# Expert buffers in existing rings, an earlier weight pool, a routing chain put out in another order, and first transfers in another order

## The chip, the cores and the metric

One core of one Trainium2 chip runs the whole program in one launch. The metric is the device time of the launch in microseconds (us); lower is better. Three runs of the kernel before gave 870.08, 864.69 and 865.5 us, median 865.5. The profiled execution, from which every row below comes, took 872.73 us, of which the profile's span is 870.9 us; the mean clock granted to TensorE in it was 0.964 of full speed.

## The reference

Attention, a dense MLP and a mixture of experts follow one another:

```python
s_g = scale * q_g @ k_all.T ; out_g = softmax(s_g) @ v_all        # 32 global tokens see all 544
mask = abs(pos[:, None] - pos[None, :]) <= 32                     # 512 local tokens: window and globals
a_l = softmax(concat([scale * q_l @ k_g.T, where(mask, s_ll, -1e9)]))
x = concat([out_g, a_l @ concat([v_g, v_l])])                     # 4 batches, 8 heads, D 64 -> [2176, 512]
h = x @ w_in ; x = (h * sigmoid(h)) @ w_out                       # 512 -> 2048 -> 512
logits = x @ w_gate ; e = argmax(logits) ; p = softmax(logits)[e] # 8 experts
eom = sigmoid(x @ w_output_gate)
out[mask_e] = p * eom[:, e] * (relu(x @ w1[e]) @ w2[e])           # 512 -> 1024 -> 512, one expert a token
```

All inputs and the output are float32.

## The kernel before

**Numbers.** A float32 product is made of three fp16 products: each operand is split into a high and a low half (`wih`/`wil` for w_in, `woh`/`wol` for w_out), scaled by a power of two taken from the sum of its squares. Such a sum is an ACT instruction that writes a tile nobody reads (`junk`) and accumulates on the side (`stat`, L226 to L228).

**Stages.** The 2176 tokens are 17 tiles of 128. Attention of batch 0 goes in float32 (`att0_s`, `att0_v`), since its operands come first and aren't split; batches 1 to 3 are split. Each step of attention computes the scores of one pair of heads, the softmax, the transposes and the product with v; `att_step` puts out one. The MLP works in groups of up to 512 tokens: `mlp_h` (L681) makes x @ w_in, `mlp_x` (L728) the second product. Attention, MLP and the preparation of weights overlap. Behind the MLP of a tile, `x2_evac` writes its split rows to a DRAM tensor `x2d`, transposes them to `x2T`, and `logits` (or `logits32` for the last tiles) computes the gates.

**Routing.** `route` turns logits into lists of rows, on DVE with small matmuls on TensorE: `onehot` and `ranks` number the tokens of each expert; `early_slots` takes the first 128 tokens of each expert among tiles 0 to 14 (`pme` L1124, then the row numbers `idge` L1125), and `last` gives, once all 17 tiles are known, the list `idg` (`pm` L1173, L1174) of 13 more slots of 128 rows whose expert is known only then. Coefficients (`pce`, `pcf`, `coef`), and the list by which results are scattered (`pt`, `ids`), come out of further small products.

**Experts.** `Moe` handles 21 slots of 128 rows in four chunks of 256 hidden units. GpSimd gathers a slot's rows (`gather`, L1241), SP transposes them (L1243), `mm_h` (L1286, L1278, L1281) makes 256 hidden units of a slot in 12 matmuls, ACT and DVE make `hb` of it, SP transposes two slots' `hb` at a time (L1313), and `mm_y` (L1323) adds the second product to `ys` in 6 matmuls. The 13 slots of `last` are gathered by `gather_late`. Weights of a chunk come as 16 tiles `ws` of 512 KB (L918), get a `stat` and are split (L954 on ACT, L955 on DVE).

**What sets the order.** A scheduler of the kernel's framework orders instructions on each engine from the source order, a priority (`tc.high_priority(URG)`) and `tc.issue_after(i)`, which holds back what it encloses until i has been put out. An engine then works in that order and waits at the first instruction whose inputs aren't there. A buffer of a ring (a pool's tag with `bufs=n`) is reused in turn: who takes it waits for the last reader of its predecessor. A pool that opens where another has closed waits for whatever used that memory. In the kernel before, `ws` has 2 buffers until `rt_ctx.close()` and 6 afterwards; the tiles of the late slots, `hb`, `r` and `ys` lie in pools opened behind `mlp_ctx.close()`.

**The start.** L1404 to L1424: SP issues q0, k0, the mask `cs`, q1, the constants `cr` (with the identity by which the softmax is transposed), w_in part 0, v0; then `scale_v0` (an ACT sum over v0, L319, and a tiny product `tot`, L192) stands ahead of the first step of attention.

Of the kernel before, what the change touches and what calls it, by code (L numbers as in the profile page):

```python
# [9 lines left out]
F32 = mybir.dt.float32  # L10
# [42 lines left out]
NEARLY = NE  # L53
ORDER = (*range(14), 16, 14, 15)
# [52 lines left out]
def tile_kernel(ctx: ExitStack, tc, csa, csr, q0, q, qn, qg, k0, k, va, vc, w_in, w_out, wg, w1, w2, out, dbg=None):  # L107
# [89 lines left out]
    woh = wto.tile([128, KF, DM], F16, name="woh")  # L197
    wol = wto.tile([128, KF, DM], F16, name="wol")
# [246 lines left out]
    pt, av, sums, xs = {}, {}, {}, {}  # L445

# [5 lines left out]
    ident = cr[:, C_ID:C_ID + 128]  # L452

# [13 lines left out]
    def att0_s(t, pr):  # L467
# [513 lines left out]
    def route(rt, rps):  # L981
# [9 lines left out]
        DVE.tensor_scalar(trib, iota, cr[:, C_P:C_P + 1], None, ALU.is_gt)  # L991
        ones = T([128, 128], "ones", BF16)
# [43 lines left out]
        apend, pc_i = [], [None]  # L1036
# [55 lines left out]
        def early(i):  # L1092
# [11 lines left out]
            else:  # L1104
# [3 lines left out]
                coef(14, 15)  # L1108

                DVE.tensor_scalar(n0[:, 1], n0[:, 1], 128.0, None, ALU.max)  # L1110
                r, SR = slice(0, 15), [128, 15, NE]
                DVE.tensor_scalar(u[:, r, 0], dhi[:, r], 0.0, None, ALU.is_equal)
                DVE.tensor_tensor(RE, ohf[:, r], bc(u[:, r], SR), ALU.mult)
                static(0, 15)

        def early_slots():
            pump_a(99)
            SR = [128, 15, NEARLY]
            for c in range(2):
                DVE.tensor_tensor(Rce[:, :, c], RE, bc(row[c][:, 0:15], SR), ALU.mult)  # L1120
            pm = rps.tile([128, NEARLY], F32, tag="av", name="pme")
            for i in range(15):
                for c in range(2):
                    PE.matmul(pm, A[:, i], Rce[:, i, c], start=(i == 0 and c == 0), stop=(i == 14 and c == 1))  # L1124
            DVE.tensor_scalar(idge, pm, -1.0, 0.0, ALU.add, ALU.max)  # L1125
# [15 lines left out]
        def last():  # L1141
            p = onehot(15, 17)
            DVE.tensor_tensor(n0[:, 2], n0[:, 1], p[:, 0, 0], ALU.add)
            n1 = T([128, NE, 1], "n1")
            DVE.tensor_tensor(n1[:, :, 0], n0[:, 2], p[:, 0, 1], ALU.add)
            cmp = d.rearrange("p i e -> p (i e)").rearrange("p (e i) -> p e i", e=NE)
            S3t = [128, NE, NT]
            DVE.tensor_tensor(cmp, bc(n1, S3t), bc(cr[:, C_CNT:C_CNT + NT].rearrange("p (a i) -> p a i", a=1), S3t), ALU.is_gt)
            sl = T([128, NE], "sl")
            DVE.tensor_reduce(sl, cmp, AX.X, ALU.add)  # L1150
            DVE.tensor_scalar(sl, sl, -float(NS), 0.0, ALU.add, ALU.max)
            DVE.tensor_tensor_scan(bnd[:, 0], one8, sl, 0.0, ALU.mult, ALU.add)
            base = T([128, 1, NE], "base")
            DVE.scalar_tensor_tensor(base[:, 0], bnd[:, 0], float(ST - NS), sl, ALU.add, ALU.subtract)
            ranks(15, 17, p, n0[:, 1:3])
            static(15, 17)
            S3 = [128, NT, NE]
            DVE.tensor_tensor(tmp, ohf, bc(base, S3), ALU.mult)
            b_ = T([128, NT, 1], "b_")
            DVE.tensor_reduce(b_[:, :, 0], tmp, AX.X, ALU.add)  # L1160
            DVE.tensor_tensor(b_[:, :, 0], b_[:, :, 0], u[:, :, 0], ALU.mult)
            DVE.tensor_tensor(b_[:, :, 0], b_[:, :, 0], dhi, ALU.add)
            SR = [128, NT, NSLOT]
            R = Rc[:, :, 2]
            i24 = iota[:, 0:NSLOT].rearrange("p (a n) -> p a n", a=1)
            DVE.tensor_tensor(R, bc(i24, SR), bc(b_, SR), ALU.is_equal)
            for c in range(2):
                DVE.tensor_tensor(Rc[:, :, c], R, bc(row[c], SR), ALU.mult)
            pump_a(99)
            pm = rps.tile([128, NSLOT], F32, tag="av", name="pm")  # L1170
# [42 lines left out]
    class Moe:  # L1213
# [376 lines left out]
```

## Time and profile before

| | before |
|---|---|
| three runs, us | 870.08, 864.69, 865.5 |
| profiled execution, us | 872.73 (span 870.9) |
| TensorE busy | 769.5 us of the span |
| DVE busy, ACT busy | 590.1 us, 516.8 us |
| first matmul, first step of the MLP, end of the MLP | 16.85, 77.66, 565.1 us |
| chunk 0 of the experts: last `mm_h` | 652.8 us |

Times in the rows are microseconds from the start of the span. PE is TensorE, SPq the queue in which SP issues transfers. A timeline row gives start, duration and count of a run of like instructions, and in brackets the idle time before it with what ended it. The table of windows gives for each stretch the busy time of each engine, the granted clock (1.00 is full speed) and the share of the 16 DMA engines that was busy; as it counts overlapping packets it can go above 1.

### The profile page before, as it was taken

The numbers are of one execution on the slowest core, as the hardware profiler recorded it, in microseconds if no ns is written. First come the engines' busy times: TensorE is split into PE (matmuls) and PEld (weight loads), VectorE is DVE, ScalarE is ACT, GpSimd is POOL, SyncE is SP. The second block draws the span as 40 slices with busy tenths as digits, with TensorE's granted clock in tenths as the row PEclk, the third lists the DMA queues.
The fourth block names the chain that finished last, engine by engine and source line by source line (L and its number), as shares of the span: only waits on it lengthen the run. The fifth ranks groups of instructions, "written<-read, shape, count | busy, mean of one in ns | idle before, by whom it ended". The sixth has DMA issues, their size and how long they took to land.

```text
span 870.9 us, 17387 instructions
## 1 busy us (share of the span) xinstructions
PE 769.5 (88%) x6201; PEld 525.3 (60%) x6201; DVE 590.1 (68%) x1649; ACT 516.8 (59%) x1017; POOL 58.1 (7%) x110
## 2 busy tenths in 40 slices
PE   2999969899899999999999889968759998899894
PEld 2898656566666766677666557545425655455541
DVE  2978876777767878767565556872126787588862
ACT  2685768677667667666545555411359846756710
POOL 0000000000000000000000000035000000000054
PEclk9999888999999999999999999979979999999997
DMA  9733444366974284646354262199975974885672
GB/s 356 292 121 123 150 149 161 107 145 167 183 122 89 48 176 99 137 86 122 67 99 106 95 146 65 46 194 194 197 202 174 237 143 151 181 167 170 141 175 90
DMA packets 182139, 127.83 MB, mean 147 GB/s; under 512 B 161437, under 2 KB 162973, under 8 KB 178592
## 3 DMA queue, kind: packets, MB, share of 16 engines
q1 hardware_dynamic: 178688, 116.67, 55.5%
q0 software_dynamic: 3360, 9.97, 3.9%
q8 instruction: 54, 0.88, 0.4%
q14 instruction: 37, 0.30, 0.1%
HBM read 76.93 MB, written 9.96 MB: 100 GB/s over the span
## 4 chain that ended last, share of the span: by engine, by line
PE 42%; DMA 20%; DVE 14%; issue 9%; ACT 9%; SPq 2%; POOL 1%; POOLq 0%; ACTq 0%; DVEq 0%
PE h L681 10%; PE x L728 10%; DMA ws<-in_w_dram 6%; PE yp L1323 5%; DMA pT<-pb 4%; DMA wil<-hb 4%; PE hp L1286 3%; PE av L531 2%; PE s L475 2%; DMA st<-in_qn_dram 2%; DVE w1b L955 2%; DVE k L210 2%; PE av L497 1%; PE av L498 1%; ACT w1b L954 1%
## 5 line engine op out<-in xcount | busy, mean ns | idle before, releaser
L728 PE MATMUL x<-woh,g 128*128 128x512 f16 x544 | 173.5, 381 | 0.3 <-ACT g L711 0.3
L681 PE MATMUL h<-xT,wih 128*128 128x256 f16 (+1 forms) x1152 | 162.0, 272 | 3.6 <-DMA xT<-xb 1.5
L681 PEld LDWEIGHTS <-wih 128*128 128x128 f16 x1152 | 109.3, 100 | 29.5 <-issue 4.7
L728 PEld LDWEIGHTS <-g 128*128 128x128 f16 x816 | 76.3, 98 | 80.4 <-issue 2.6
L1323 PE MATMUL yp<-w2b,wil 128*128 (+1 forms) x384 | 93.4, 390 | 19.5 <-DMA wil<-hb 11.9
L728 PE MATMUL x<-wol,g 128*128 128x512 f16 x272 | 103.8, 382 | 0.0
L1286 PE MATMUL hp<-w1b,x 128*128 128x256 f16 (+1 forms) x672 | 87.8, 279 | 8.9 <-DMA x<-xg 4.7
L681 PE MATMUL h<-xT,wil 128*128 128x256 f16 (+1 forms) x576 | 87.3, 273 | 0.0
L1286 PEld LDWEIGHTS <-x 128*128 128x128 f16 x672 | 67.0, 101 | 27.6 <-issue 5.9
L464 ACT ACTIVATE e<-e,mx,esc 128x192 f32<-128x192 f32 (+1 forms) x128 | 70.5, 553 | 19.1 <-DVE mx L461 17.5
L228 ACT ACTIVATE junk<-ws 128x1024 f16<-128x1024 f32 x48 | 50.8, 1058 | 41.5 <-DMA ws<-in_w_dram 40.8
L1323 PEld LDWEIGHTS <-wil 128*128 128x128 f16 x384 | 38.0, 102 | 61.4 <-issue 13.4
L683 ACT ACTIVATE tanh<-h,th 128x512 f32<-128x512 f32 (+1 forms) x72 | 47.1, 658 | 41.9 <-PE h L681 41.7
L700 ACT ACTIVATE g<-tanh,i_out 128x512 f16<-128x512 f32 (+1 forms) x64 | 44.1, 692 | 33.8 <-DVE tanh L696 33.7
L681 PEld LDWEIGHTS <-wil 128*128 128x128 f16 x576 | 55.4, 100 | 7.2 <-issue 0.2
L701 DVE SCALAR_TENSOR_TENSOR g<-tanh,i_out,g 128x512 f16<-128x512 f32 (+1 forms) x64 | 45.7, 716 | 20.5 <-ACT g L700 20.3
L696 DVE SCALAR_TENSOR_TENSOR tanh<-tanh,h 128x512 f32<-128x512 f32 (+1 forms) x64 | 41.4, 649 | 26.6 <-ACT tanh L683 26.3
L460 DVE CUSTOM_DVE_ANT_0 e<-s,cs 128x192 f32<-128x192 f32 (+1 forms) x128 | 42.7, 370 | 19.7 <-PE s L450 11.0
L955 DVE SCALAR_TENSOR_TENSOR w1b<-ws,s,w1b 128x1024 f16<-128x1024 f32 x32 | 40.1, 1280 | 14.1 <-ACT w1b L954 14.0
L955 DVE SCALAR_TENSOR_TENSOR w2b<-ws,s,w2b 128x1024 f16<-128x1024 f32 x32 | 40.6, 1282 | 12.0 <-ACT w2b L954 9.5
L516 DVE SCALAR_TENSOR_TENSOR pb<-e,pb 128x384 f16<-128x384 f32 (+1 forms) x48 | 28.0, 587 | 18.6 <-ACT pb L515 18.2
L514 POOL MEMSET pb<- 128x256 f16 (+1 forms) x48 | 12.4, 259 | 360.9 <-DMA pT<-pb 144.6
(345 smaller groups left out, 1395.1 us busy)
## 6 DMA issues: line engine op xcount, KB each, us to landing
ws<-in_w_dram SPq DMA_DIRECT2D x64, 512.0 KB
st<-in_w_out_dram SPq DMA_DIRECT2D x8, 1024.0 KB
st<-in_w_in_dram SPq DMA_DIRECT2D x6, 1024.0 KB
q<-in_q_dram SPq DMA_DIRECT2D x12, 512.0 KB
x2d<-x2s SPq DMA_DIRECT2D x17, 256.0 KB
st<-in_k_dram SPq DMA_DIRECT2D x3, 1088.0 KB
st<-in_qn_dram SPq DMA_DIRECT2D x3, 1024.0 KB
st<-in_va_dram SPq DMA_DIRECT2D x3, 1024.0 KB
```

What stands on the lines that cost most here:

```text
L228: ACT.activation(junk, x, ACTF.Square, accum_out=m)
L460: DVE.tensor_tensor_reduce(dst[:, hh, 0:wt], ps[:, hh, 0:wt], mask, 1.0, -3e38, ALU.add, ALU.max, mx[:, hh:hh + 1])
L464: ACT.activation(dst[:, hh, 0:wt], dst[:, hh, 0:wt], ACTF.Exp, scale=esc[:, b:b + 1], bias=mx[:, 2 + hh:3 + hh], accum_out=sums[i][:, h:h ...
L681: PE.matmul(ps[:, f], w[:, kk, c], xj[:, l + kk, 0:n], start=(m == 0 and kk == 0), stop=(m == 2 and kk == KD - 1))
L683: pin[0] = ACT.activation(t, ps, ACTF.Tanh, scale=th[:, b:b + 1])
L696: pin[1] = DVE.scalar_tensor_tensor(t, t, 1.0, ps, ALU.add, ALU.mult)
L700: ACT.activation(hi, t, ACTF.Copy, scale=i)
L701: pin[2] = DVE.scalar_tensor_tensor(lo, t, i, hi, ALU.mult, ALU.subtract)
L728: PE.matmul(x2ps[2 * j + c], x[:, f, o], w[:, ff], start=(ff == 0 and m == 0), stop=(ff == KF - 1 and m == 2))
L955: DVE.scalar_tensor_tensor(d[:, 1], t[a], sc_, d[:, 0], ALU.mult, ALU.subtract)
L1286: PE.matmul(ps[:, 0], x[:, xl + kk], self.rows("1", n, l, kk), start=(m == 0 and kk == 0), stop=(m == 2 and kk == KD - 1))
L1323: PE.matmul(ps, h[:, hl + j], self.rows("2", n, l, j), start=(m == 0 and j == 0), stop=(m == 2 and j == KJ - 1))
```

## The change

- **Start.** The mask and k0 come in parts, w_in part 0, `cr` and the first half of v0 are issued ahead of w_in part 1, q1 and the rest; `scale_v0` is put out behind the fourth step of attention.
- **Weights.** `ws` has 6 buffers from the end of attention on, and six of the eight w1 tiles of chunk 1 are asked for ahead of the routing of the last tiles (`prefetch(wq1)`).
- **Memory.** The MLP's pools stay open. Late rows are gathered into the `xt` and `x2` rings (`room`), transposed into `woh` and `wol` (`xlate`); `ys` of ten late slots share those rings; `hb` and the `junk` of later weights go in the MLP's `g` ring of 6, `r` in its ring of 2 (before: own rings of 2 and 3, and one own `junk`). Routing tables lie in halves of `wil`, `ohs` and `ohb`.
- **Routing.** `early_slots` up to `idge`, and `last` up to `idg`, are put out at high priority; coefficients and the scatter list come behind `idge` and `idg` by `issue_after`.

```diff
 def load_k0():
-        SP.dma_start(kt[0], k0)
+        for h in range(0, 4, 2):
+            SP.dma_start(kt[0][:, h:h + 2], k0[:, h:h + 2])
...
         load_q(0)
+        SP.dma_start(cs[:, 0:WT[0]], csa[:, 0:WT[0]])
         load_k0()
-        SP.dma_start(cs, csa)
+        load_w(("i", 0))
+        SP.dma_start(cr, csr)
+        load_v0()
+        load_w(("i", 1))
         load_q(1)
-        SP.dma_start(cr, csr)
-        load_w(("i", 0))
-        load_v0()
+        SP.dma_start(cs[:, WT[0]:], csa[:, WT[0]:])
+        load_v0_rest()
+        load_w(("i", 2))
...
-        scale_v0()
         while npos[0] < P["n0"]:
             att_step()
+            if npos[0] == 4:
+                with tc.issue_after(sc0[0].ins):
+                    scale_v0()
...
-        def early_slots():
-            pump_a(99)
+        def early_slots():
+            SR = [128, 15, NEARLY]
+            with tc.high_priority(URG):
+                pump_a(99)
...
+                key_i[0] = DVE.tensor_scalar(idge, pm, -1.0, 0.0, ALU.add, ALU.max)
+            with tc.issue_after(key_i[0].ins):
+                DVE.tensor_scalar(n0[:, 1], n0[:, 1], 128.0, None, ALU.max)
+                coef(14, 15)
                 static(0, 15)
...
         def last():
-            p = onehot(15, 17)
+            with tc.high_priority(URG):
+                p = onehot(15, 17)
...
+                key_i[0] = DVE.tensor_scalar(idg, pm, -1.0, 0.0, ALU.add, ALU.max)
+            with tc.issue_after(key_i[0].ins):
+                early_coefs()
...
+        def room(self, k, a):
+            if k < 6:
+                if k % 2 == 0:
+                    self.pair[a] = xt_p.tile([128, 2, DM], F32, tag="xT", name="yx")
+                return self.pair[a][:, k % 2]
+            if k < 10:
+                return x2_p.tile([128, DM], F32, tag=("x2s", "x2T")[k % 2], name="yx")
+            return self.ys_p.tile([128, DM], F32, tag=f"y{k}", name="yx")
+
+        def xlate(self, k):
+            return xlv[k // 8][:, k % 8]
...
-                r = self.pools[1].tile([128, CH], F32, tag="r", name="r")
-                if o == 0:
-                    self.hb[q] = self.pools[1].tile([128, 2, 2, CH], F16, tag="hb", name="hb", bufs=2)
...
+            r = gt_p.tile([128, CH], F32, tag="tanh", name="r")
+            if o == 0:
+                self.hb[q] = g_p.tile([128, 2, 2, CH], F16, tag="g", name="hb")
...
-                    wm["s"], wm["n"] = rt_ctx.enter_context(tc.tile_pool(name="ws", bufs=2, side="right")), 1
+                    wm["s"], wm["n"] = ctx.enter_context(tc.tile_pool(name="ws", bufs=6, side="right")), 3
...
+        wm["j"] = lambda: g_p.tile([128, 1024], F16, tag="g", name="junk")
+        wq1 = [(1, "1", p) for p in range(4)]
+        prefetch(wq1)
         moe.mm_h(0)
...
         rt_ctx.close()
-        mlp_ctx.close()
-
         ys_p = ctx.enter_context(tc.tile_pool(name="ys", bufs=1))
-        xs_p = ctx.enter_context(tc.tile_pool(name="xs", bufs=1))
-        r_p = ctx.enter_context(tc.tile_pool(name="r", bufs=3))
-        wm["s"], wm["n"] = ctx.enter_context(tc.tile_pool(name="ws", bufs=6, side="right")), 3
-        wm["j"] = lambda: xs_p.tile([128, 1024], F16, tag="xg", name="junk", bufs=1)
```

The new order of SP's transfers at the start. Before:

```order
L256 DMA q_166<-in_q_dram 128x512
L269 DMA k_168<-in_k_dram 128x2176
L1408 DMA cs<-in_csa_dram 128x608
L256 DMA q_171<-in_q_dram 128x512
L1410 DMA cr<-in_csr_dram 128x590
L375 DMA st<-in_w_in_dram 128x1024
L307 DMA v_176<-in_va_dram 128x2048
```

And now:

```order
L256 DMA q_167<-in_q_dram 128x512
L1427 DMA cs<-in_csa_dram 128x192
L270 DMA k_170<-in_k_dram 128x1088 x2
L379 DMA st<-in_w_in_dram 128x1024
L1430 DMA cr<-in_csr_dram 128x590
L308 DMA v_176<-in_va_dram 128x1024
L379 DMA st<-in_w_in_dram 128x1024
L256 DMA q_180<-in_q_dram 128x512
L1434 DMA cs<-in_csa_dram 128x416
L311 DMA v_176<-in_va_dram 128x1024
```

q1, two thirds of the mask and half of v0 moved behind two parts of w_in.

TensorE at the start of the program (`tot<-vm` belongs to `scale_v0`, `s` are scores, `h<-cr,e` transposes by the identity). Before:

```order
L192 MATMUL tot<-vm,cr 128x1
L475 MATMUL s<-k_168,q_166 128x192 x2
L192 MATMUL tot<-tm,cr 128x1
L192 MATMUL tot<-vm,cr 128x1 x2
L475 MATMUL s<-k_168,q_166 128x192 x4
L489 MATMUL h<-cr,e 128x128
```

And now:

```order
L481 MATMUL s<-k_170,q_167 128x192 x8
L496 MATMUL h<-cr,e 128x128
L497 MATMUL h<-cr,e 64x128
L496 MATMUL h<-cr,e 128x128
L497 MATMUL h<-cr,e 64x128
```

`tot<-vm` headed the engine's order; now it comes behind the first twelve products with v.

SP from the last weights of chunk 0 to the end of the late transposes (`x<-xg` are early and late gathered rows before; now `x<-xg` early, `woh<-yx` and `wol<-yx` late; `wil<-hb` transposes hidden units). Before:

```order
L918 DMA ws<-in_w_dram 128x1024 x2
L1243 DMA_TRANSPOSE x<-xg 128x8x128 x4
L752 DMA x2d<-x2s 128x1024 x2
L1243 DMA_TRANSPOSE x<-xg 128x8x128
L1537 TENSOR_LOAD eidx
L1537 ISA x2
L1243 DMA_TRANSPOSE x<-xg 128x8x128 x2
L1313 DMA_TRANSPOSE wil<-hb 128x8x128
L1243 DMA_TRANSPOSE x<-xg 128x8x128
L1313 DMA_TRANSPOSE wil<-hb 128x8x128 x3
L1243 DMA_TRANSPOSE x<-xg 128x8x128 x13
L918 DMA ws<-in_w_dram 128x1024 x6
```

And now:

```order
L925 DMA ws<-in_w_dram 128x1024 x14
L758 DMA_TRANSPOSE x2T<-x2s 128x8x128
L759 DMA x2d<-x2s 128x1024
L758 DMA_TRANSPOSE x2T<-x2s 128x8x128
L759 DMA x2d<-x2s 128x1024
L925 DMA ws<-in_w_dram 128x1024 x2
L759 DMA x2d<-x2s 128x1024
L1260 DMA_TRANSPOSE x<-xg 128x8x128 x8
L759 DMA x2d<-x2s 128x1024 x2
L1344 DMA_TRANSPOSE wil<-hb 128x8x128 x3
L1260 DMA_TRANSPOSE woh<-yx 128x8x128
L1344 DMA_TRANSPOSE wil<-hb 128x8x128
```

The six loads of chunk 1 left their place behind the thirteen late transposes and stand among the last `x2T` transposes, and all eight early transposes stand ahead of the last two `x2d` writes. On TensorE the 30 small products `pme` stood behind the last matmul of the MLP; now 35 of L688 (`mlp_h`) and 60 of L735 (`mlp_x`) come behind them.

## Rows read from the trace of the kernel before

**Rows 1.** The page: its span, and among the costliest groups the sums over weights.

```profile
span 870.9 us, 17387 instructions
...
L228 ACT ACTIVATE junk<-ws 128x1024 f16<-128x1024 f32 x48 | 50.8, 1058 | 41.5 <-DMA ws<-in_w_dram 40.8
```

**Rows 2.** Stretch, length; PE, PEld, DVE, ACT, POOL busy; clock; DMA share; GB/s.

```profile
0.00:17.40 17.40, 0.55 (x3) 0.54 (x3) 3.14 (x3) 3.89 (x4) 0.47 (x10) 1.00 0.92 338
17.40:77.70 60.30, 59.87 (x240) 53.53 (x240) 51.79 (x139) 41.73 (x105) 0.10 (x1) 1.00 0.58 216
...
455.00:565.10 110.10, 103.93 (x833) 70.11 (x832) 70.70 (x221) 63.50 (x100) 0.33 (x2) 0.98 0.35 93
565.10:594.40 29.30, 20.96 (x234) 17.02 (x231) 20.78 (x110) 5.58 (x13) 8.61 (x9) 0.77 0.93 180
594.40:652.80 58.40, 38.98 (x219) 20.73 (x218) 11.58 (x36) 21.16 (x42) 12.31 (x13) 0.88 0.96 203
```

**Rows 3.** Timeline of the start, all engines.

```profile
0.74 0.40 SPq L256 DMA_DIRECT2D q<-in_q_dram  x1
...
11.34 0.69 DVE L381 TENSOR_SCALAR woh<-st 128x1024 int32<-128x1024 int32 x1 [11.34 <-DMA st<-in_w_in_dram]
...
14.79 1.91 ACT L319 ACTIVATE junk<-v 128x2048 f16<-128x2048 f32 x1 [12.77 <-DMA v<-in_va_dram]
...
16.85 0.58 PE L192 MATMUL tot<-vm,cr 128*128 128x1 f32 x2 [16.85 <-ACT junk L319]
...
17.36 1.00 PE L475 MATMUL s<-k,q 64*128 64x192 f32 x2
```

**Rows 4.** Timeline of TensorE round the first step of the MLP.

```profile
77.66 0.42 PE L681 MATMUL h<-xT,wih 128*128 128x256 f16 x1
```

**Rows 5.** Timeline of TensorE from the end of the MLP through chunk 0.

```profile
564.92 0.90 PE L1124 MATMUL pme<-Rc,A 128*128 128x8 bf16 x30
...
575.26 7.67 PE L1286 MATMUL hp<-w1b,x 128*128 128x256 f16 x48 [2.34 <-DMA x<-xg]
584.41 1.30 PE L1173 MATMUL pm<-Rc,A 128*128 128x31 bf16 x34 [1.48 <-DVE cp L1069]
...
643.05 7.25 PE L1323 MATMUL yp<-w2b,wil 128*128 x22 [10.46 <-DMA wil<-hb]
650.14 1.47 PE L1286 MATMUL hp<-w1b,x 128*128 x12
...
652.89 2.53 PE L1323 MATMUL yp<-w2b,wil 128*128 x11
```

**Rows 6.** Timeline of GpSimd: the gathers.

```profile
567.20 1.12 POOL L1241 DMA_INDIRECT xg<-x2d,idge  x1 [108.51 <-DVE cf L1071]
...
593.99 0.95 POOL L1241 DMA_INDIRECT xg<-x2d,idg  x1 [10.66 <-DVE hb L1305]
...
609.43 0.95 POOL L1241 DMA_INDIRECT xg<-x2d,idg  x1 [0.30 <-issue]
```

**Rows 7.** Timeline of SP's queue from the last weights of chunk 0.

```profile
542.71 1.52 SPq L918 DMA_DIRECT2D ws<-in_w_dram  x2
570.69 7.27 SPq L1243 DMA_TRANSPOSE x<-xg  x4
...
602.76 26.93 SPq L1243 DMA_TRANSPOSE x<-xg  x13
629.86 3.26 SPq L918 DMA_DIRECT2D ws<-in_w_dram  x6
633.22 13.83 SPq L1313 DMA_TRANSPOSE wil<-hb  x4
```

**Rows 8.** Timeline of DVE: the late list.

```profile
586.34 0.18 DVE L1174 TENSOR_SCALAR idg<-pm 128x31 int32<-128x31 f32 x1
```

**Rows 9.** What TensorE waited for, 455 to 565.1 us: total, times, longest.

```profile
PE s L784 <- DMA x2T<-x2s: 2.5, 1, 2.5
```

**Rows 10.** The same, 652.8 to 870.9 us.

```profile
PE tot L192 <- ACT junk L228: 5.1, 6, 2.8
```

More of the change, by code (lines that the diff above doesn't have):

```diff
@@ L1159, in last @@
[L1159 to L1168, printed above, removed]
@@ L1169, in last @@
-            pump_a(99)
-            pm = rps.tile([128, NSLOT], F32, tag="av", name="pm")
-            for i in range(NT):
-                for c in range(2):
-                    pm_i = PE.matmul(pm, A[:, i], Rc[:, i, c], start=(i == 0 and c == 0), stop=(i == NT - 1 and c == 1))
-            DVE.tensor_scalar(idg, pm, -1.0, 0.0, ALU.add, ALU.max)
-            for c in range(2):
-                DVE.tensor_tensor(Rc[:, :, c], R, bc(row[2 + c], SR), ALU.mult)
-            pm = rps.tile([128, NSLOT], F32, tag="av", name="pt")
@@ L1178, in last @@
-            for i in range(NT):
-                for c in range(2):
-                    PE.matmul(pm, A[:, i], Rc[:, i, c], start=(i == 0 and c == 0), stop=(i == NT - 1 and c == 1))
-            ohr = oh.rearrange("p i e -> p (i e)")
-            vf = ohr[:, 0:2 * NSLOT].rearrange("p (a n) -> p a n", a=2)
-            DVE.tensor_scalar(vf[:, 1], pm, 0.0, float(BIG), ALU.is_equal, ALU.mult)
-            DVE.tensor_scalar(vf[:, 1], vf[:, 1], -1.0, None, ALU.add)
-            DVE.tensor_tensor(ids, vf[:, 1], pm, ALU.add)
@@ L1240, in gather @@
         def gather(self, n, s, src, rows, t, x):
-            POOL.indirect_dma_start(out=t[:, :], out_offset=None, in_=x2d[0:rows, :],
+            POOL.indirect_dma_start(out=t, out_offset=None, in_=x2d[0:rows, :],
                                     in_offset=bass.IndirectOffsetOnAxis(ap=src[:, s:s + 1], axis=0))
@@ new lines, in rest @@
+                for kd in ("1", "2"):
+                    busy = c > 0 or kd == "2"
+                    for n in [n for n in self.order if c or n >= (ne if kd == "1" else ny)] + [None]:
+                        if n is not None:
+                            if kd == "1":
+                                self.mm_h(n)
+                            else:
+                                self.mm_y(c, n)
+                        while busy:
+                            if wpend or cur:
+                                pump_w(cur, P["KS"])
+                            else:
+                                busy = False
+                                if kd == "1":
+                                    self.coefs(c)
+                                cur = [(c + 1, "21"[kd == "1"], p) for p in range(4)] if c + 1 < NCH else []
+                                prefetch(cur)
+                            if n is not None:
+                                break
```

245 lines of the change are left out of this document (125 added, 120 removed).

## The prediction, made before the run

> **What bounds the kernel now.** I read the page first [rows 1]: in a span of 870.9 us TensorE is busy 88%, so what can be won is TensorE's idle time and little else. The table of windows [rows 2] says where that idle time lies, and it was read next. In the first 17.4 us TensorE works 0.55 us. From there to the first step of the MLP it works 59.87 of 60.30 us: batch 0 is bound by TensorE, with DVE close behind at 51.79. From 455 to 565.1 us, where the MLP ends (T below), 6.2 us of 110.1 are idle. From 565.1 to 652.8 us, chunk 0 of the experts, TensorE works 20.96 + 38.98 = 59.9 us of 87.7 and so idles 27.8 us, at a mean granted clock of 0.77 and 0.88, between its two levels, against 0.98 in the stretch ahead; the DMA share there is 0.93 and 0.96. Behind 652.8 us follow three chunks that are mostly full. The change can gain at the two idle places, the start (16.8 us) and chunk 0 (27.8 us). Timelines of these two places were read last.
>
> **The start.** The first matmul is the small `tot<-vm` of `scale_v0` at 16.85 us; it waited 16.85 us for ACT's sum over v0, which began at 14.79 when v0 had landed, and the scores behind it on TensorE began at 17.36 [rows 3]. None of them needs it. Ahead of v0's end SP had asked for q0, k0, mask, q1, constants, w_in part 0 and v0: 0.26 + 1.11 + 0.31 + 0.26 + 0.30 + 1.05 + 1.05 MB. The 3.30 MB up to w_in part 0 had landed at 11.34 [rows 3]; with some 2 us until data flow that is an estimated 0.354 MB/us. By this line the new order brings q0, the first third of the mask and k0 (1.47 MB) at 6.2 us, w_in part 0 (2.52 MB) at 9.1 instead of 11.34, the constants at 10.0, half of v0 at 11.5, w_in part 1 at 14.4, q1 at 15.2, and the rest of v0 at 17.4. So the first eight scores (some 2 us) start at 6.2 instead of 17.36, the transposes at 10, the products with v at 11.5; by the time at which TensorE began in the kernel before, some 7 us of its 60 us of work are done. Then it waits for nothing new: q1 is there, and the sum over v0, now about 3 us later, is behind twelve products with v. Since TensorE works 59.87 of 60.30 us up to the MLP, a lead is kept to 77.66 us [rows 4], unless DVE holds it: DVE starts its conversions 2.2 us earlier, and its softmax 11 us earlier. The term is **-7 us**. Its bounds: -3, if DVE's conversions of w_in (2.2 us earlier, and little more) set the first step of the MLP; -10, if nearly all of the 11.2 us from 17.36 to 6.2 is kept.
>
> **Weights of chunk 0, 455 to 565 us.** Six buffers instead of two let SP ask for `ws` tiles ahead of need, and the six tiles of chunk 1 come here, where the DMA share is 0.35 [rows 2]; the last load of chunk 0 went out at 542.71 [rows 7]. A full ring makes SP wait with `x2T` transposes behind the loads, and TensorE has already waited 2.5 us for such a transpose [rows 9]. `pme` now stands ahead of 35 matmuls of `mlp_h` and 60 of `mlp_x`; if DVE's chain in front of it is late, TensorE waits in order, which no row prices. I take 0 from bounds of -3 (that wait goes) and +5 (it doubles at two transposes); the nearest row is the 2.5.
>
> **Chunk 0.** Five things of the kernel before stand in its path. `pme` ran at 564.92, at the end of the MLP, the first early gather at 567.20, the first `hp` at 575.26 behind an idle 2.34 us [rows 5, 6]. The late list came at 586.34 [rows 8], T+21.2; the first late gather waited until 593.99 for the memory of `hb` [rows 6]. The thirteen transposes held SP for 26.93 us from 602.76, then the six loads of chunk 1 for 3.26 us, and only at 633.22 the next transposes of `hb`, for which TensorE stood idle 10.46 us until 643.05 [rows 5, 7].
>
> In the new order 35 matmuls of 0.109 us and 60 of 0.216 us, 16.8 us of the MLP, come behind `pme` (a matmul of 256 columns is 1.30/12 us, one of 512 columns 2.36/11 us, by the rows at 650.14 and 652.89 less 0.17 us of latency [rows 5]). So the eight early slots are gathered and transposed while the MLP still runs, and their eight `mm_h` follow T at once. On DVE the coefficients (about sixteen instructions of some 0.16 us, as short as the list's own 0.18 [rows 8]) leave the chain to the late list: 2.6 us off, T+18.6. The late gathers follow it directly, at T+18.6 instead of T+28.9, into rings that the MLP has left. At 1.25 us a gather ((609.43 - 593.99)/12 = 1.29 with issue) and 2.07 us a transpose, the transposes end at about T+18.6 + 3.5 + 26.9 = T+49, the last lands at T+54; with the `hb` transposes of the eight early slots between them I take T+60. TensorE's own work is 21 x 1.30 for `mm_h`, 21 x 1.30 for `mm_y` and an estimated 7 us of routing products (the gates and five products up to the 1.30 us of `pm` [rows 5]), 62 us. The order keeps 14 of the 21 `mm_y` behind the last `mm_h`; before, 9.3 were left. So chunk 0 ends at T+60 + 14 x 1.30 = T+78; before, it ended by the same count at 652.8 + 9.3 x 1.30 = 664.9, T+99.8. The term is **-22 us**, between -10 (the next rival) and -30 (T+70: TensorE's 62 us and 8 us of waits). That SP's `hb` transposes no longer stand behind loads is in it, not on top.
>
> **Chunks 1 to 3.** Work and order are nearly the same. A sum over weights now takes a slot of the `g` ring that `hb` uses; `r` has 2 buffers for 3, `hb` up to 6 for 2. TensorE's waits for these sums were 5.1 us in all [rows 10]. I take 0, with bounds of -5 (they vanish) and +5 (they double). New memory for the routing tables, one idle copy of the identity on DVE, and the rewritten loop cost nothing: the copy lies beside DVE's idle time.
>
> **The sum** is -7 + 0 - 22 + 0 = -29 us, against the profiled execution's 872.73. That execution lies 7.2 us above the median of 865.5 and above all three runs; the terms are differences, so they are taken off the median: **836 us**. The forecast's own range is 825 to 848.
>
> **Rivals.**
>
> *The start's lead is lost.* DVE works 51.79 us of 60.30 up to the MLP [rows 2], and the first step of the MLP needs its split of w_in. If DVE sets it, the start gives 0 to -2 and the time is 843. Against it: DVE idles 14 of the first 17.4 us, and gets work earlier now. Chance 0.12.
>
> *Transfers set chunk 0.* The two windows moved 29.3 x 0.180 + 58.4 x 0.203 = 17.1 MB at a DMA share near 1 [rows 2]. Without the six loads (3.1 MB) 14.0 MB remain; at the same 0.195 MB/us these are 72 us, the last `mm_h` comes at T+72, and 14 `mm_y` later chunk 0 ends at T+90: -10 us, 848 us. Against it: eight of the 21 gathers with their transposes now lie ahead of T, and the gather wait at 593.99 was for memory, not for a transfer. Chance 0.15. The Trainium skill (DMA: Bandwidth & Descriptors, Issuing engines are not separate DMA queues) says that transfers started by different engines run on the same 16 DMA engines and interleave, so that other issuers save only their own issue time; by that rule this rival would hold whole, and 848 would be the time. The DMA share near 1 agrees with it; that TensorE was stopped by one transpose behind loads in one queue speaks for order rather than volume.
>
> *The change doesn't bring what it says.* SP waits in order: sixteen loads stand among the last `x2T` and `x2d` transfers, two of them ahead of the last `x2d` that the early gathers read. If the ring is full there, logits, `pme` and the gathers come as late as before, TensorE stops at `pme`, and what is won behind T is lost ahead of it; only the start is left less some 4 us, 862 us, within what counts as no change. For it: the loads of chunk 0 ran to 542.71 already [rows 7]. Chance 0.11.
>
> *Slower: sums over weights stall in the shared ring.* ACT makes 48 such sums of 1058 ns [rows 1], in order with the `r` and `hb` work that TensorE waits for. A `junk` tile now waits for the transpose of the `hb` six places ahead; such a transpose held SP 13.83/4 = 3.5 us each in a crowded stretch [rows 7]. If each sum is held 0.6 us, the 29 us are gone; at 0.9 us the loss is 43 us and the time 865.5 - 29 + 43 = 879. It decides from 0.8 us a sum. Against it: six places are some 8 us of `mm_h`, and ACT already idles 41.5 us ahead of these sums for the load [rows 1], so a held slot is mostly hidden. Chance 0.09.
>
> **How the numbers follow.** The forecast has 0.53. A difference of 1% (8.7 us) is about what a measurement of this kernel can tell from none: faster is below 856.8, slower above 874.2. The forecast and the first two rivals are faster: 0.80; the third is no change, 0.11; the fourth slower, 0.09. The range leaves out the last two, which are 0.20, and takes in the bounds of the sum as far as they are likely together: 818 (-10, -30, and 7 us in the other two terms) to 858 (-3 and -10, with 5 us lost elsewhere).
>
> **What would show it.** In the profile of the changed kernel: first scores near 6 us, and the first step of the MLP near 70 instead of 77.66; T near 558; the first early gather some 14 us ahead of T; eight `mm_h` in one piece behind T with no wait for gathered rows; the first late gather at T+18 to T+20, waiting for the list and not for memory; no wait of 10 us for `wil<-hb`; the last `mm_h` of chunk 0 near T+60; DMA share near 1 in a shorter stretch. The prediction fails if TensorE waits at `pme` or for `x2T` for more than 5 us, if T keeps its 565, or if ACT's idle time ahead of the sums is put down to SP's `hb` transposes rather than loads.

## The result, and the profile after

The changed kernel took 838.58 us in the median of four runs (835.22 to 844.86) against 865.1 us of before; the ratio is 0.969, interval 0.963 to 0.975. The forecast of 836 us lay 2.6 us off. The profiled execution took 837.55 us, span 835.7. T, the end of the MLP, is 561.3 us (565.1 before), and from T to the end of the span the kernel takes 274.4 us instead of 305.8. So 31 of the 35 us by which the spans differ lie behind T, and 4 ahead of it. The profiled execution of before took 872.73 us, 7.6 us above its median, so the parts that are read from the two profiles add up to 35 us and not to the 26.5 us between the medians.

The busy time by stretch, in the columns of [rows 2], cut at the first step of the MLP, at 455 us, at 561.15 (0.2 us ahead of T, where TensorE's next product starts) and at the last `mm_h` of chunk 0:

```profile
0.00:17.40 17.40, 9.25 (x34) 7.17 (x34) 7.28 (x27) 6.67 (x18) 0.65 (x12) 1.00 0.88 316
17.40:69.60 52.20, 52.20 (x209) 48.89 (x209) 45.22 (x115) 36.32 (x85) 0.10 (x1) 1.00 0.75 257
69.60:455.00 385.40, 358.48 (x3551) 251.67 (x3550) 285.72 (x800) 253.89 (x534) 14.09 (x55) 0.96 0.55 118
455.00:561.15 106.15, 100.56 (x839) 68.22 (x837) 70.73 (x219) 65.62 (x107) 7.78 (x8) 1.00 0.57 162
561.15:623.05 61.90, 48.69 (x390) 33.52 (x389) 32.62 (x140) 16.76 (x38) 12.95 (x13) 0.89 0.90 166
623.05:835.70 212.65, 189.80 (x1187) 115.87 (x1184) 156.19 (x354) 135.09 (x237) 21.62 (x21) 0.98 0.68 169
```

The idle time of TensorE in chunk 0 is 61.9 - 48.7 = 13.2 us, where it was 27.8; the granted clock is 0.89 there, where it was 0.77 and 0.88. But the row from 69.60 to 455 is 8.1 us longer than its like of before:

```profile
77.70:455.00 377.30, 356.77 (x3534) 251.01 (x3533) 280.74 (x790) 251.85 (x528) 14.09 (x55) 0.97 0.55 122
```

Not all of the gain behind T is idle time. The same 1400 matmuls of the experts (`hp` and `yp`) keep TensorE busy for 241.4 us where they took 248.1, at a mean granted clock behind T of 0.96 instead of 0.94.

TensorE's timeline of the changed kernel, to be read beside [rows 3 to 5]:

```profile
6.16 1.61 PE L481 MATMUL s<-k,q 64*128 64x192 f32 x4 [6.16 <-DMA k<-in_k_dram]
...
69.58 0.84 PE L688 MATMUL h<-xT,wih 128*128 128x256 f16 x3
...
543.63 0.90 PE L1130 MATMUL pme<-ohs,A 128*128 128x8 bf16 x30
...
561.15 0.60 PE L773 MATMUL x2t<-cr,x2f 128*128 128x128 f32 x4
...
563.45 1.47 PE L1325 MATMUL hp<-w1b,x 128*128 128x256 f16 x12
...
568.03 8.02 PE L1325 MATMUL hp<-w1b,x 128*128 128x256 f16 x72
...
596.18 1.86 PE L1317 MATMUL hp<-w1b,woh 128*128 x4 [5.33 <-DMA woh<-yx]
...
605.97 4.45 PE L1325 MATMUL hp<-w1b,woh 128*128 x24 [4.04 <-DMA woh<-yx]
...
622.62 0.60 PE L1320 MATMUL hp<-w1b,wol 128*128 x4
623.05 0.81 PE L1354 MATMUL yp<-w2b,wil 128*128 128x512 f16 x3
```

GpSimd's gathers, beside [rows 6]:

```profile
545.02 1.12 POOL L1258 DMA_INDIRECT xg<-x2d,idge  x1 [111.88 <-DVE tmp L1067]
...
577.40 0.95 POOL L1258 DMA_INDIRECT yx<-x2d,idg  x1 [17.04 <-DVE idg L1188]
...
593.06 0.95 POOL L1258 DMA_INDIRECT yx<-x2d,idg  x1 [0.30 <-issue]
```

SP's queue, beside [rows 7]:

```profile
510.34 0.88 SPq L925 DMA_DIRECT2D ws<-in_w_dram  x2
...
548.46 16.02 SPq L1260 DMA_TRANSPOSE x<-xg  x8
...
585.27 25.49 SPq L1260 DMA_TRANSPOSE woh<-yx  x7
...
619.09 4.83 SPq L1344 DMA_TRANSPOSE wil<-hb  x3
...
629.35 9.86 SPq L925 DMA_DIRECT2D ws<-in_w_dram  x6
```

First scores at 6.16 us; `pme` at 543.63, 17.7 us ahead of T; all eight early gathers ahead of T; eight `mm_h` from T+2.1 to T+14.7 that wait for no gathered row; the first late gather at T+16.1, waiting for the list. The last `mm_h` of chunk 0 ends at T+62. No transpose of hidden units stops TensorE in this stretch; it waits 5.33 and 4.04 us for late rows instead. ACT's idle time ahead of the 48 sums over weights, 41.5 us in [rows 1], is 17.2 us on the page of the changed kernel, and loads still end it:

```profile
L228 ACT ACTIVATE junk<-ws 128x1024 f16<-128x1024 f32 x48 | 50.5, 1052 | 17.2 <-DMA ws<-in_w_dram 17.1
```

In what follows one execution of e4, which took 1100.8 us at a granted clock of 0.67, is left out of its median, which is 853.4 us where x2's expectation speaks of 854.

### The profile page after: what moved, and what is told of

The parts are those of the page before. It is cut to its first block, busy times and chain, and to the rows that moved or that the text cites. A ratio compares the mean times of both kernels' runs of the same rounds, so it can differ in the third digit from the quotient of the medians.

```text
span 835.7 us, 17394 instructions
## 1 busy us (share of the span) xinstructions
PE 759.0 (91%) x6201; PEld 525.3 (63%) x6201; DVE 597.8 (72%) x1650; ACT 514.3 (62%) x1017; POOL 57.2 (7%) x110
## 4 chain that ended last, share of the span: by engine, by line
PE 63%; DMA 16%; DVE 9%; ACT 6%; issue 5%; SPq 1%; POOLq 0%; ACTq 0%; DVEq 0%
PE h L688 16%; PE x L735 14%; PE yp L1354 9%; PE hp L1325 5%; DMA ws<-in_w_dram 4%; DMA pT<-pb 4%; PE av L538 3%; PE hp L1317 3%; PE s L481 3%; DMA woh<-yx 2%; PE av L505 2%; PE av L504 2%; DMA xT<-xb 1%; PE hp L1320 1%; DVE w1b L962 1%
## 5 line engine op out<-in xcount | busy, mean ns | idle before, releaser
L735 PE MATMUL x<-woh,g 128*128 128x512 f16 x544 | 172.1, 379 | 3.6 <-ACT g L718 1.5
L688 PE MATMUL h<-xT,wih 128*128 128x256 f16 (+1 forms) x1152 | 161.6, 273 | 10.6 <-DMA xT<-xb 5.4
L688 PEld LDWEIGHTS <-wih 128*128 128x128 f16 x1152 | 108.7, 100 | 35.2 <-DMA xT<-xb 5.8
L735 PEld LDWEIGHTS <-g 128*128 128x128 f16 x816 | 76.3, 98 | 85.0 <-issue 2.4
L735 PE MATMUL x<-wol,g 128*128 128x512 f16 x272 | 103.1, 379 | 0.0
L688 PE MATMUL h<-xT,wil 128*128 128x256 f16 (+1 forms) x576 | 89.0, 274 | 0.0
L228 ACT ACTIVATE junk<-ws 128x1024 f16<-128x1024 f32 x48 | 50.5, 1052 | 17.2 <-DMA ws<-in_w_dram 17.1
L688 PEld LDWEIGHTS <-wil 128*128 128x128 f16 x576 | 54.8, 101 | 7.7 <-issue 0.4
L708 DVE SCALAR_TENSOR_TENSOR g<-tanh,i_out,g 128x512 f16<-128x512 f32 (+1 forms) x64 | 45.5, 712 | 18.2 <-ACT g L707 18.2
L703 DVE SCALAR_TENSOR_TENSOR tanh<-tanh,h 128x512 f32<-128x512 f32 (+1 forms) x64 | 41.5, 649 | 18.9 <-ACT tanh L690 18.6
L962 DVE SCALAR_TENSOR_TENSOR w1b<-ws,s,w1b 128x1024 f16<-128x1024 f32 x32 | 40.4, 1280 | 18.8 <-ACT w1b L961 18.8
L1325 PE MATMUL hp<-w1b,x 128*128 128x256 f16 x384 | 47.1, 272 | 4.3 <-ACT r L1338 4.3
L1325 PEld LDWEIGHTS <-x 128*128 128x128 f16 x384 | 37.7, 100 | 12.3 <-issue 4.7
L1338 ACT ACTIVATE r<-hp 128x256 f32<-128x256 f32 x56 | 20.5, 379 | 29.7 <-PE hp L1325 19.8
## 6 DMA issues: line engine op xcount, KB each, us to landing
st<-in_w_in_dram SPq DMA_DIRECT2D x6, 1024.0 KB, 12.4
```

The costliest lines, as they stand in the source:

```text
L228: ACT.activation(junk, x, ACTF.Square, accum_out=m)
L688: PE.matmul(ps[:, f], w[:, kk, c], xj[:, l + kk, 0:n], start=(m == 0 and kk == 0), stop=(m == 2 and kk == KD - 1))
L703: pin[1] = DVE.scalar_tensor_tensor(t, t, 1.0, ps, ALU.add, ALU.mult)
L708: pin[2] = DVE.scalar_tensor_tensor(lo, t, i, hi, ALU.mult, ALU.subtract)
L735: PE.matmul(x2ps[2 * j + c], x[:, f, o], w[:, ff], start=(ff == 0 and m == 0), stop=(ff == KF - 1 and m == 2))
L962: DVE.scalar_tensor_tensor(d[:, 1], t[a], sc_, d[:, 0], ALU.mult, ALU.subtract)
```

## The experiments

All were timed in five rounds beside the kernel before; the changed kernel itself was run again with the second set. The runs fall into three sets, each on another chip: e1, e2, e3 and e7, beside which the kernel before took 864.2 us; a1, e4, e5 and e8, with 864.9; x1, x2, e6 and b1, with 867.5. Runs of different sets are therefore best compared by their ratios. T is read from each profile; "tail" is from T to the end of the span.

| run | median us | ratio to before, interval | T | tail |
|---|---|---|---|---|
| changed kernel | 838.6 | 0.969, 0.963 to 0.975 | 561.3 | 274.4 |
| a1 changed, again | 835.4 | 0.965, 0.961 to 0.969 | 563.7 | 270.8 |
| e1 old start | 834.7 | 0.965, 0.962 to 0.969 | 561.4 | 268.4 |
| e2 before, new start only | 860.1 | 0.994, 0.991 to 0.998 | 560.2 | 297.6 |
| e3 old routing text | 829.1 | 0.960, 0.955 to 0.965 | 561.1 | 266.7 |
| e8 old start, old routing text | 840.2 | 0.968, 0.962 to 0.973 | 565.7 | 273.6 |
| e7 ring of two | 856.3 | 0.989, 0.985 to 0.993 | 560.7 | 295.9 |
| e4 chunk-1 loads late | 853.4 | 0.986, 0.981 to 0.990 | 563.9 | 287.8 |
| x2 loads late, sums behind | 849.0 | 0.978, 0.975 to 0.982 | 565.0 | 284.1 |
| x1 before, sums behind | 872.1 | 1.004, 1.001 to 1.007 | 562.8 | 307.0 |
| e5 seven slots turned on TensorE | 840.7 | 0.973, 0.969 to 0.977 | 556.4 | 278.6 |
| e6 own junk tile | 833.7 | 0.960, 0.957 to 0.963 | 562.3 | 269.6 |
| b1 two more early mm_y | 836.0 | 0.965, 0.962 to 0.968 | 559.7 | 271.3 |

> The changed kernel once more, unedited, beside the runs with which it is compared. If the new start is worth nothing or costs something in this kernel (the run with the old start took 834.7 us, and reached the end of the MLP at the same 561.3 us), it takes 836 to 840 us; if the 3.9 us between the two were drift from one set of runs to the other, 833 to 836 us.

a1 took 835.4 us, with e1's ratio: the 3.9 us were drift from one set to the other. The two medians of the changed kernel differ by 3.2 us, and the intervals reach some 3.5 us either way, so differences below some 5 us between these runs are not told apart.

**The start, undone and alone (e1, e2).**

```diff
-        SP.dma_start(cs[:, 0:WT[0]], csa[:, 0:WT[0]])
...
+        load_k0()
+        SP.dma_start(cs, csa)
+        load_q(1)
+        SP.dma_start(cr, csr)
+        load_w(("i", 0))
+        load_v0()
...
+        scale_v0()
```

> The changed kernel with the start of the kernel before: transfers in the old order and whole, the sum over v0 ahead of attention. Theory (the lead of 8.1 us at the first step of the MLP is won, and some 4 us of what the trace shows lost up to the end of the MLP come from other parts of the change): 8 us slower than the changed kernel, 846 us, end of the MLP at 569. Rival (attention and MLP give half of any lead back, since at the end of the MLP the changed kernel leads by 4.0 us only): 4 us slower, 842 us, end of the MLP at 565. Both: first step of the MLP at 77 to 78 us.

> The kernel before with the new start and nothing else of the change. Theory (the lead is kept): first step of the MLP near 69.6 us, end of the MLP at 557, 8 us faster than before, 857 us. Rival (half is given back in attention and MLP): end of the MLP at 561, 4 us faster, 861 us.

Neither number of e1 came. With the old start its first step of the MLP is at 77.88 us, 8.3 us behind the changed kernel's 69.58; yet T is 561.35 against 561.3, and the ratio is that of a1. In the kernel before, the new start alone gave 0.6% (0.2 to 0.9), 5 us, with T at 560.15: the rival's size. Nearly all of the lead goes at one place. Timeline of TensorE in the changed kernel:

```profile
120.51 1.13 PE L573 MATMUL s<-k,qgs 64*32 64x272 f32 x8 [5.66 <-DVE tb L180]
...
126.96 1.03 PE L688 MATMUL h<-xT,wih 128*128 128x256 f16 x4 [5.01 <-DMA xT<-xb]
```

and in the run with the old start:

```profile
121.61 1.02 PE L569 MATMUL s<-k,qgs 64*32 64x272 f32 x8 [2.48 <-DVE tb L180]
...
128.81 1.01 PE L192 MATMUL tot<-qm,cr 128*128 128x2 f32 x4 [2.05 <-ACT ge L577]
```

The scores of the global tokens come at 120.5 and 121.6 us: they wait for `tb`, in DVE's order, where the preparation of w_out's last parts ends at about the same time with either start (118.4 and 117.0 us in DVE's timeline). The two waits, 10.7 us in all, stand against 4.5 us with the old start. Up to 115 us TensorE has done 530 matmuls against 494 with the old start, up to 132 us 564 against 562. The windows of the two (columns as above) show the place, and that the granted clock is lower there with the new start; changed kernel, then old start:

```profile
115.00:132.00 17.00, 6.48 (x34) 3.76 (x35) 11.07 (x31) 12.48 (x24) 0.28 (x1) 0.51 0.66 205
```

```profile
115.00:132.00 17.00, 10.77 (x68) 7.04 (x68) 13.19 (x42) 14.39 (x29) 0.31 (x1) 0.70 0.61 204
```

**The routing chain as written before (e3), and with the old start too (e8).** The edit puts the old text of `early_slots` and `last` back, without priority.

```diff
-            with tc.high_priority(URG):
-                pump_a(99)
+            pump_a(99)
...
-            with tc.issue_after(key_i[0].ins):
-                early_coefs()
```

> The changed kernel with the routing chain written as before: no high priority, coefficients and static lists in their old places ahead of the lists of rows. The order still has the first list's products with 33 and 60 matmuls of the MLP behind them. Theory (the early start of the experts doesn't come from the priority; only some coefficients come back into the chain to the late list): 2 to 4 us slower than the changed kernel, 841 to 843 us, late list at T+18 to T+20 instead of T+16. Rival (the priority is what makes the early slots early): the first gather again at T+2, 12 to 20 us slower, 851 to 859 us.

> The changed kernel with both the start and the routing text of the kernel before; memory, ring and loads of chunk 1 stay. If the two gains found apart (3.9 and 9.5 us) are separate, 825 us. If they are the same gain (late rows land a little earlier or TensorE has more to do while they come), 828 to 831 us. If the old start's run was drift, 829 us.

The rival of e3 is out: the first gather stays 16.3 us ahead of T. So the priority isn't what makes the early slots early. The late list is 2.7 us later (first late gather at T+18.8), as expected, but no time is lost by it: e3's ratio is 0.5% below a1's and e8's 0.2% above, with intervals that overlap. The new order of the chain is worth nothing that these runs can measure.

**The ring of six and its early loads, undone (e7), and the loads alone (e4).**

```diff
-  wm["s"], wm["n"] = ctx.enter_context(tc.tile_pool(name="ws", bufs=6, side="right")), 3
+  wm["s"], wm["n"] = rt_ctx.enter_context(tc.tile_pool(name="ws", bufs=2, side="right")), 1
```

> The changed kernel with the weights' ring of 2 buffers until routing is done and of 6 behind it, and the first loads of chunk 1 there, as before; memory, routing text and start stay new. In its order the first list's products stand behind the last matmul of the MLP again. Theory (six buffers, not the priority, are what brings the early slots ahead of T): first gather at T+2, eight mm_h at T+10 to T+28, 12 to 20 us slower than the changed kernel, 851 to 859 us. Rival (transfers set chunk 0 whatever the early slots do): last mm_h of chunk 0 within 4 us of T+62, 3 to 6 us slower, 842 to 845 us.

```diff
-        prefetch(wq1)
         moe.mm_h(0)
...
+            if ne:
+                with tc.issue_after(self.tr.ins):
+                    prefetch(cur)
```

> The changed kernel with six buffers from the end of attention on, but with the first six loads of chunk 1 asked for only behind the last late transpose, as before; SP's order has them ahead of four transposes of hidden units again. Theory (these loads were half of the stop of 10.5 us at the transposes of hidden units): 4 to 8 us slower than the changed kernel, 843 to 847 us, with TensorE waiting for wil<-hb behind the loads. Rival (the loads are hidden beside 14 mm_y; what the ring of six gives is early slots alone): 0 to 2 us, 838 to 840 us.

e7 lost 20.9 us against a1 (2.4% by the ratios), by its theory and a little over it: first gather at T+1.8, first `mm_h` at T+11.9. But e4 keeps the early slots (first gather T-16.2, eight `mm_h` at once) and loses 17.9 us (2.0%) all the same, two to four times what its theory gave. The loads of chunk 1 are late in e7 too, but e7 loses its time elsewhere. What TensorE waited for behind T in e7 (total, times, longest), then its last long wait, SP's first loads of chunk 1 and ACT's first sum over them:

```profile
PE yp L1354 <- DMA wil<-hb: 19.0, 4, 9.1
PE hp L1325 <- DMA x<-xg: 9.6, 3, 5.0
```

```profile
612.51 2.74 PE L1354 MATMUL yp<-w2b,wil 128*128 128x512 f16 x6 [9.12 <-DMA wil<-hb]
...
617.82 3.19 SPq L925 DMA_DIRECT2D ws<-in_w_dram  x6
...
625.38 1.05 ACT L228 ACTIVATE junk<-ws 128x1024 f16<-128x1024 f32 x1
```

TensorE's waits for early rows and the two long ones for transposed hidden units, 24.2 us in all, were over at 612.5, before SP asked for the first of these loads, and ACT's sum did not wait for it. Counted as the prediction counts (the last `mm_h` of chunk 0, and 1.30 us for each `mm_y` that is left behind it), the profiles divide up as follows; "rest" is from there to the end of the span.

| run | T | last `mm_h` of chunk 0 | `mm_y` left | chunk 0 ends | rest |
|---|---|---|---|---|---|
| before | 565.1 | T+87.8 | 9.3 | T+100.0 | 205.8 |
| x1 | 562.8 | T+85.1 | 9.3 | T+97.2 | 209.8 |
| e2 | 560.2 | T+86.4 | 9.3 | T+98.6 | 199.0 |
| e7 | 560.7 | T+88.8 | 12.0 | T+104.4 | 191.5 |
| e4 | 563.9 | T+74.7 | 13.0 | T+91.6 | 196.2 |
| x2 | 565.0 | T+60.1 | 14.5 | T+79.0 | 205.1 |
| changed | 561.3 | T+61.9 | 14.5 | T+80.7 | 193.7 |
| a1 | 563.7 | T+59.0 | 14.5 | T+77.8 | 193.0 |

e7 loses all of its time in chunk 0, by early slots that come late; behind it, it is no slower than the changed kernel. So the early slots and the early loads are both needed: with late loads alone (e4) 18 us go, with late slots as well (e7) 21, by waits of different kinds, and the two worths don't add up. What early loads give beside late slots no run shows.

How late loads hurt is in the timeline of e4, ACT and TensorE:

```profile
621.35 1.06 ACT L228 ACTIVATE junk<-ws 128x1024 f16<-128x1024 f32 x1 [5.45 <-DMA ws<-in_w_dram]
...
626.26 0.70 ACT L1335 ACTIVATE hb<-r 128x256 f16<-128x256 f32 x2
...
597.17 2.72 PE L1354 MATMUL yp<-w2b,wil 128*128 128x512 f16 x6 [12.64 <-ACT wih L1362]
...
627.59 4.44 PE L1325 MATMUL hp<-w1b,woh 128*128 x24 [12.41 <-ACT r L1338]
```

ACT's sums over the late loads stand ahead of `hb` in ACT's order. ACT waits 5.45 us for the first load and makes four sums, and TensorE waits 12.41 us behind it. (The 12.64 us are not of this edit: a1 has the like, see the last section.)

**The sums alone (x1, x2).** In both, the sums over these loads stand behind the last `hb` of chunk 0; x1's edit:

```diff
-                                prefetch(wq1)
+                                prefetch(wq1, c > 0)
...
+                        with tc.issue_after(self.hbi.ins) if c == 0 else ExitStack():
+                            pump_w(wq1, P["KS"])
```

> The kernel before, with one thing moved: ACT's sums over the first loads of chunk 1 stand behind the last hidden units of chunk 0 in ACT's order, instead of ahead of five of them. SP's order stays: six loads, then the four transposes of hidden units for which TensorE waited 10.46 us. Theory (in the trace of before ACT waited 6.88 us for the loads and made six sums, 627.5 to 642.6 us, with hidden units of chunk 0 queued behind; that, not SP's order, was the stop): the wait falls to 2 to 4 us, 7 to 12 us faster than before, 853 to 858 us. Rival (SP's loads ahead of the transposes were the stop): the wait stays near 10 us and the time at 863 to 866 us.

> The changed kernel with the six loads of chunk 1 late, as in the run that took 854 us, but with the sums over them behind the hidden units of chunk 0 on ACT. Theory (of the 18.6 us which late loads cost, the 12.4 us in which TensorE waited for ACT are these sums in ACT's order): 840 to 844 us, no wait over 4 us of mm_h for r. Rival (the transfers themselves cost it: six loads of 512 KB among the late rows and the hidden units): 850 to 855 us.

The theory of x1 was formed on these rows of ACT in the kernel before, and fell:

```profile
627.10 0.38 ACT L1304 ACTIVATE r<-hp 128x256 f32<-128x256 f32 x1 [0.94 <-PE hp L1286]
634.36 1.06 ACT L228 ACTIVATE junk<-ws 128x1024 f16<-128x1024 f32 x1 [6.88 <-DMA ws<-in_w_dram]
...
643.00 0.72 ACT L1301 ACTIVATE hb<-r 128x256 f16<-128x256 f32 x2 [0.22 <-DMA wil<-hb]
```

With the sums out of the way ACT waited longer, for the transposes themselves (timeline of x1, ACT, TensorE and SP):

```profile
638.38 0.72 ACT L1303 ACTIVATE hb<-r 128x256 f16<-128x256 f32 x2 [15.78 <-DMA wil<-hb]
...
649.25 1.05 ACT L228 ACTIVATE junk<-ws 128x1024 f16<-128x1024 f32 x1
...
638.44 6.83 PE L1325 MATMUL yp<-w2b,wil 128*128 x22 [10.84 <-DMA wil<-hb]
...
625.92 2.95 SPq L918 DMA_DIRECT2D ws<-in_w_dram  x6
628.97 13.36 SPq L1315 DMA_TRANSPOSE wil<-hb  x4
```

The wait of 10.46 us [rows 5] was there again with 10.84. In the kernel before, the first of four transposes behind six loads was late, and `hb`, with its ring of 2, waited for it too; the sums were not the stop, and the time was 0.4% above that of before (0.1 to 0.7). The rival's wait came, but its time did not: x1 took 872.1 us, with 867.5 for the kernel before in the same set. That the loads ahead of the transposes made them late, as the prediction had it, agrees with this and isn't shown by it alone: no run took only the loads away there. x2 has a ring of 6 for `hb`, and there the sums do count: 4 to 6 us less than e4 (849.0 against 853.4 us; ratios 0.978 against 0.986, intervals that overlap by 0.1%), no wait for `r` over 4 us, and the last `mm_h` of chunk 0 at T+60, as in the changed kernel, where e4 has T+75. That the ring makes the difference to x1 is argued. But 11 us to a1 by the ratios, 13.6 by the medians, remain, against both numbers, and by the table they lie behind chunk 0. Up to T+130 TensorE waited 5.7 us in two pieces for transposes of hidden units, in a1 not at all, and its idle time from T+60 to T+130 is 11.1 us against 3.8 in a1, which fits weights of chunk 1 that come late.

**Do transfers set chunk 0 (e5)?**

```diff
-TURN = ()
+TURN = (0, 2, 4, 6, 8, 10, 12)
```

> The changed kernel with seven of the thirteen late slots transposed by TensorE (8 matmuls of 128 columns each, and one copy out of PSUM on DVE or ACT) instead of by SP's DMA transposes, by the branch that the change brought and left unused. Theory (DMA transposes set when late rows land: 25.5 us for seven of them on SP, waits of 5.3 and 4.0 us for them on TensorE): 4 to 8 us faster than the changed kernel, 830 to 834 us. Rival (the gathers, 9 us each to land, or the DVE's order set it): no gain, 838 to 842 us.

The rival came. The first 60 us behind T in e5, then in a1:

```profile
556.37:616.37 60.00, 45.51 (x435) 34.23 (x434) 35.68 (x145) 16.38 (x37) 12.54 (x13) 0.89 0.61 142
```

```profile
563.74:623.74 60.00, 46.07 (x397) 32.99 (x395) 32.99 (x143) 17.46 (x40) 12.64 (x13) 0.86 0.92 171
```

The DMA share falls from 0.92 to 0.61, and with seven transposes off the DMA engines chunk 0 isn't shorter: its last `mm_h` comes at T+61.4, in a1 at T+59.0. (3.8 of the 45.5 us of TensorE's busy time are the transposes themselves.) x2 has a share of 1.00 up to the same place, T+60.1, so the share doesn't tell what holds chunk 0. But the profiles of e5 and a1 both have the stop of the last section, 12.4 and 11.9 us on TensorE, and neither waits for a late row behind it. What the transposes cost where that stop is absent, e5 doesn't show.

**A tile of its own for the sums (e6), two more early products (b1).**

```diff
+        jk = ys_p.tile([128, 1024], F16, tag="junk", name="junk")
+        wm["j"] = lambda: jk
```

> The changed kernel with a tile of its own for the sums' unused output from the end of routing on, as before, instead of slots of the g ring. Theory (slots of the shared ring hold nothing up): 834 to 838 us, as the changed kernel. Rival (the sums wait for slots, or hidden units for sums, by the prediction's fourth rival): 4 us or more faster, 832 us or less.

```diff
-nye=6
+nye=8
```

> The changed kernel with all eight mm_y of the early slots, instead of six, put out ahead of the late rows (nye 8 for 6). Theory (TensorE waits some 9 us for late rows in chunk 0 and has 14 mm_y left behind them; two of them fill 2.6 us of the wait): 2 to 4 us faster than the changed kernel, 832 to 834 us. Rival (what is filled here is missing behind, where mm_y cover the conversions of chunk 1): no gain, 835 to 838 us.

e6's ratio lies 0.5% below a1's, with intervals that overlap, and its 833.7 us lie between the two numbers: a small cost of the shared ring is possible, a large one is not. b1 is a1's time: its rival. No run shows a version that is clear of the changed kernel on the fast side; e3 and e6 come nearest.

## Why the prediction was right, and where its steps were not

**The sum** was -29 us and the measured difference 26.5 us, but two terms stood in for each other. In the profiles of before and after, which differ by 35 us, the part up to T gave -4 for a forecast of -7, chunk 0 -19 for -22, and the three chunks behind it -12 for 0. That the sum came within 3 us is in part luck.

**The start, -7.** The step itself came: first scores at 6.16 us for 6.2, first step of the MLP at 69.58 for 70. What failed is "a lead is kept": the term was checked up to the first step of the MLP and no further, and 40 us later DVE's order held both kernels. In the changed kernel it is worth nothing that a1 against e1 can show (each ratio is known within 0.4%), alone in the old one 5 us. The first rival had the right engine and the wrong place.

**Weights of chunk 0, 0.** No wait at `pme` and none of size for `x2T`. T in e1 is 3.7 us ahead of before without any lead from the start; but x1, which up to T is the kernel before, has T at 562.8 where before has 565.1, and over all profiles of changed kernels T lies between 556 and 566 us. That is too wide to say that the rest of the change gives anything here. T came at 561.3 where 558 was foretold.

**Chunk 0, -22.** Nearly each date came (T-16 for T-14, T+16.1 for T+18.6, T+62 for T+60), and by the prediction's own count the chunk ends at T+81 (a1: T+78) where T+78 was foretold. The early slots' part is borne out by e7, which has them behind T and ends the chunk at T+104. What the term had wrong is the part of the early loads. They were put "in it, not on top", by way of SP's order; e4 shows that without them 11 of the 19 us of chunk 0 are gone, and by another way, ACT's sums. With the sums moved (x2) chunk 0 is as short as in the changed kernel, though the loads stand ahead of the transposes. So the size was right, and the way in which late loads hurt this kernel was not; for the kernel before x1 rules out the sums and leaves SP's order standing. The term also counts each product at one speed; the rise of the granted clock (6.7 us of TensorE's busy time behind T) is in no term.

**Chunks 1 to 3, 0.** By the same count these take 193.7 us for 205.8 before, -12, outside the bounds of 5 in these two profiles: this term was mis-sized the most, together with the start. The profiles scatter: with the old memory before, x1 and e2 have 199 to 210 us, with the new one the changed kernel, a1, e4 and e7 have 191 to 196, and x2, whose loads are late, 205, so that the gain here may be anything from 5 to 16 us. TensorE's idle time behind the last `mm_h` of chunk 0 is 22.9 us, before 29.7. The waits from T+130 to the end are now:

```profile
PE hp L1325 <- ACT r L1338: 4.3, 3, 1.9
PE yp L1354 <- DMA wil<-hb: 3.6, 2, 2.1
PE hp L1317 <- ACT r L1338: 0.9, 1, 0.9
PE tot L192 <- ACT junk L228: 0.8, 1, 0.8
```

From the last `mm_h` of chunk 0 on the waits for sums are 4.7 us, nearly the 5.1 of before [rows 10], but only 0.8 us of them come behind T+130; 4.6 us in which `mm_y` waited for DVE (L1337) are gone. That the memory does it is argued from this grouping; no run changed it alone.

**The rivals.** Transfers as the bound of chunk 0 would have left -10, and chunk 0 gave -19 to -22; e5 took a third off the DMA share without a gain, though its profile has the stop that hides late rows. The Trainium skill's rule that transfers of all issuers share the 16 DMA engines (DMA: Bandwidth & Descriptors, Issuing engines are not separate DMA queues) is not contradicted by that; what these runs don't bear out is that the time follows from it. The slower rival's place was real, its cause wasn't: sums do hold up hidden units in ACT's order (12.41 us in e4) when their loads are late, while slots of the shared ring cost at most some 0.5% (e6).

## What to carry to other kernels

Ask for the next stage's weights before the stretch in which transfers are dense, and count what stands behind each load on every engine: its transposes in SP's order and its sums in ACT's. Follow a lead past the next place where another engine's order holds the work, or it counts twice. When a sum comes out right, undo its parts one by one, and then look where each run lost its time: here two parts each cost most of the gain when they were missing, by different waits, so that their worths can't be added.

## What the runs showed that was not expected

In a1, e4, e5, x2, e6 and b1 DVE stands about 10 us in front of the same list (`ids`, lines L1199 to L1201), for a cause that the trace doesn't name; in the first changed run, e1, e3 and e7 it doesn't, and e8 has 6.1 us a little behind it. All six profiles with the stop are of the second and third set of runs; with one profile a run, chance isn't excluded. Timeline of a1:

```profile
594.33 0.19 DVE L1199 TENSOR_SCALAR oh<-pt 128x31 f32<-128x31 f32 x1 [10.05 <-remote]
```

TensorE then waits 11.9 us for ACT's first results, and not for late rows; the changed kernel waits 5.33, 4.04 and 2.6 us instead and takes the same time within 0.5%. A stop of 10 us there costs little, since it falls in time in which TensorE would have waited for late rows. What causes it stays open.
